# A fused linear-attention and MoE kernel: the first token block of expert 0 loaded as plain rows and turned on TensorE, and two second-visit scatters of group 1 put behind the last two of group 0

## The chip, the cores and the metric

The kernel runs on one core of a Trainium2 chip. The metric is the device time of one execution in microseconds (us); lower is better. A core has five engines with instruction streams of their own: PE (TensorE, matrix products), ACT (ScalarE), DVE (VectorE), POOL (GpSimd) and SP (SyncE, which here only issues transfers). Transfers run on 16 DMA engines. Each engine takes its instructions in the order of the program, so an instruction that waits holds back everything behind it on its engine.

## The reference

Linear attention without a causal mask, and a mixture of experts with noisy top-2 routing on its result:

```
q, k = phi(q), phi(k)                    # phi(x) = elu(x) + 1;  8 batches, 8 heads, 576 positions, 64 wide
kv = einsum('bhsd,bhse->bhde', k, v);  z = sum_s k
x = (q @ kv) / (q @ z + 1e-6)            # as 4608 tokens x 512
noisy = x @ w_gate + log1p(exp(x @ w_noise)) * noise        # 4608 x 8 experts
top2 = the two largest of a row;  w = softmax over these two
for e in range(8):                       # w1[e] 512 x 1024, w2[e] 1024 x 512
    for k in range(2):
        rows = top2[:, k] == e
        out[rows] += w[rows, k] * (relu(x[rows] @ w1[e]) @ w2[e])
```

`argpartition(-noisy, 2)` does not order the two best by their size: the kernel visits a token first for one of its two experts ("first visit", F) and then for the other ("second visit", S).

## The kernel before, in words

**Attention.** The batches go in four groups g = 0 to 3 of two. For a group, `K.g.h` are the kv products (L216, operand `e` = phi(k) and `v`), `V` their eviction into `kvbd` (L228), `T`/`t` a transpose of kv and its copy `kvt` (L235, L240), `U`/`u` the product with the router's weights and its copy (L246, L252). `Q.g.i` turns a piece of q on TensorE (L262) and `q.g.i` is ACT's copy of it to `pqt` (L267). `N.g.t` is the product of q with kv for a third t of the group (24 matmuls, L278), and `n.g.t.*` is DVE's work on it: the reciprocal of the denominator (L287, L289), the normalised rows into `xr` (L293) and the router's partial sums (L300).

**Routing.** Five units u (group 0, 1, 2, and group 3 in two parts). `R.u` is one step of the function `route`; it ends with the place of every token in a list in DRAM, `x_sorted`. `D.u.sl.ci` scatters 128 rows of unit u (1152 bytes each, sl = 0 first and 1 second visits) from `xr` to `x_sorted`: one indirect DMA of POOL (L413) and a memset behind it (L405). `xr` has three buffers, for groups 0 and 3, for group 1, and for group 2.

**Experts.** A block is a piece of one expert's list: "0a" is expert 0, first visits, tiles 0 and 1 (256 rows), "0b" its tiles 2 and 3, "1a" and "2a" the first of experts 1 and 2. `W.e.i` loads 1 MB of weights (L464, POOL), `M.k` the routing data of a block (L471, SP), `X.k` its rows (SP): turned by the transfer into `xt` (L615) or as rows `xn` (L617), according to the tuple `PLAIN`. A block of rows is turned on TensorE by `G.k.h` (L641, into PSUM, and a copy to `xt`, L645). `H.k.fc` is an eighth of the first product (4 matmuls, L697) and its ReLU on ACT (L699) into `hT`; `Y.k.t` is the second product of a tile (8 matmuls, L711), `y.k.t` its eviction on DVE (L723) and the store of it (L733).

**Order.** Everything up to expert 0's last block stands in one hand-written list of words, `SCRIPT`. Each word issues its instructions on all engines at once, and the order of the words is the order on each engine. At the word `^` the pools `A_kq` and `A_v` (q, k and v) are given back, and pools that are opened later lie in their place; at `|` the attention's pools go.

**PSUM.** Until `|` there are four small PSUM tiles of 2 KB per partition: two of the pool `ps_misc` (name `misc`) and two of `ps_b` (name `b`). `K`, `T`, `U`, `Q` and `R` take theirs from the method `misc()`, which gives the two pools in turn:

```
pool, name = self.ps_misc[self.turn % len(self.ps_misc)]
self.turn += 1
```

`H` and `Y` take theirs from `ps_b` alone, with the same buffers as the `b` of `misc()`. The word `one` makes `misc()` use `ps_misc` only from there on.

Of the kernel before, what the change touches and what calls it, by code (L numbers as in the profile page):

```python
# [860 lines left out]
R.2 n.2.2.2 R.2 R.2 R.2 R.2 R.2 t.3 m.q3.0 ^ X.0a W.1.1 D.1.0.8 D.1.1.5 D.1.0.3 D.1.0.7 D.1.0.4 D.1.1.3 D.0.1.7
D.0.1.8 H.0a.7 R.2 R.2 H.0a.2 H.0a.3 R.2 H.0a.4 Q.3.0 q.3.0 R.2 H.0a.5 U.3 u.3 Q.3.1 H.0a.0 H.0a.1 H.0a.6 R.2 R.2 R.2
q.3.1 R.2 R.2 R.2 n.2.2.1 R.2 N.3.0 R.2 R.2 R.2 Q.3.4 Q.3.2 q.3.2 R.2 R.2 R.2 Q.3.3 n.3.0.0 n.3.0.2 n.3.0.4 n.3.0.3
n.3.0.1 one D.1.1.4 D.2.1.1 D.2.0.7 D.2.0.6 D.2.1.0 D.2.0.0 W.2.0 D.2.0.5 N.3.1 R.2 M.2a X.0b X.1a q.3.3 H.0b.7 Y.0a.0
H.0b.0 q.3.4 n.3.1.0 n.3.1.2 n.3.1.4 R.2 n.3.1.1 n.3.1.3 X.2a M.0b y.0a.0 R.3 H.0b.6 N.3.2 H.0b.3 n.3.2.0 R.3 n.3.2.2
R.3 Y.0a.1 n.3.2.1 R.3 R.3 R.3 H.0b.2 R.3 y.0a.1 H.1a.2 H.1a.3 R.3 n.3.2.3 R.3 n.3.2.4 D.2.0.1 D.2.0.4 D.1.1.2 W.2.1 |
M.1a D.2.1.4 R.3 R.3 R.3 R.3 R.3 H.1a.0 H.0b.5 R.3 H.1a.4 R.3 R.3 R.3 H.0b.1 R.3 R.3 H.0b.4 R.3 R.3 R.3 R.3 R.3 R.3
H.1a.6 R.3 R.3 D.3.0.1 D.2.0.3 D.2.0.8 D.2.0.2 D.3.0.2 D.1.1.6 D.3.0.3 D.3.0.0 D.3.1.2 R.4 R.4 H.1a.5 R.4 R.4 Y.0b.1
Y.0b.0 R.4 R.4 R.4 H.2a.2 y.0b.0 y.0b.1 R.4 R.4 R.4 X.3a R.4 R.4 H.2a.0 R.4 H.1a.7 H.1a.1 R.4 R.4 H.2a.3 H.2a.1 Y.1a.0
R.4 X.0c Y.1a.1 H.2a.6 R.4 R.4 H.2a.5 R.4 y.1a.0 R.4 X.1b M.1b M.3a X.2b R.4 H.2a.4 R.4 R.4 R.4 H.2a.7 Y.2a.0 R.4 R.4  # L870
y.1a.1 M.0c y.2a.0 D.4.0.1 D.4.0.0 D.1.1.7 D.3.0.5 D.3.1.3 D.1.1.1 W.3.0 D.2.1.6 D.4.0.2 D.4.1.1 D.4.1.0 D.3.0.4
D.3.1.1 W.3.1 Y.2a.1 Y.1a.2 H.0c.5 M.2b y.2a.1 R.4 H.1b.3 H.1b.2 H.1b.4 H.0c.0 H.1b.7 H.0c.1 H.0c.3 H.0c.2 H.0c.4
H.0c.6 H.0c.7 X.0d G.2b.0 Y.0c.0 R.4 y.1a.2 Y.0c.1 y.0c.1 y.0c.0 H.1b.1 H.1b.6 H.1b.5 H.1b.0 H.2b.1 H.2b.4 H.2b.6
G.3a.0 Y.1b.1 Y.1b.0 H.2b.7 G.3a.1 H.2b.3 H.2b.0 H.3a.5 H.3a.1 H.3a.4 y.1b.1 y.1b.0 H.2b.5 H.2b.2 H.3a.3 Y.2b.0 G.0d.0
# [255 lines left out]
```

## Time and profile before

| | |
|---|---|
| median of 3 runs | 406.09 us (405.78 to 409.9) |
| profiled execution | 404.67 us, span 402.9 us |
| busy time, PE | 343.6 us (85% of the span) |
| busy time, POOL | 267.9 us (66%) |
| busy time, DVE | 186.0 us (46%) |
| busy time, ACT | 181.6 us (45%) |
| DMA | 85.60 MB, mean 212 GB/s |

The span runs from the first to the last instruction in the profile; the execution's own time has 1.8 us around it. Engines overlap, so the shares don't add up. "PEclk" is the clock that TensorE was granted, as a share of full speed. In a timeline a line is one or several instructions of one kind in a row; its first number is the start in us from the beginning of the span, the second how long they took. In brackets stands how long the engine was idle ahead of it, and what it waited for.

### The profile page before, as it was taken

Reading aid. Unit: us, or ns where it says so; the run is one execution under the profiler, and the core shown is the slowest. Engines: PE = TensorE matmul, PEld = TensorE weight load, DVE = VectorE, ACT = ScalarE, POOL = GpSimd, SP = SyncE. Lnnn points to the kernel's source line nnn. Section 1 sums busy time; section 2 is a strip of 40 time slices with the busy share of each in tenths; the row PEclk is TensorE's granted clock in tenths of the full one; section 3 lists DMA queues with packets and bytes.
Section 4 is the critical chain, followed back from the end, with each engine's and each line's share of the span. In section 5 each row is a group of like instructions: output and inputs, shape, how many; then the busy total and the mean of one; then the engine's idle time right before and its main releaser. Section 6 shows DMA issues by size and latency. Waiting matters only on the chain.

```text
span 402.9 us, 7018 instructions
## 1 busy us (share of the span) xinstructions
PE 343.6 (85%) x2527; PEld 204.1 (51%) x2557; DVE 186.0 (46%) x506; ACT 181.6 (45%) x342; POOL 267.9 (66%) x405
## 2 busy tenths in 40 slices
PE   6972757637378999989999999999999999999991
PEld 2452646526265657655566556545544544564440
DVE  3646969995839752331454233142224232343130
ACT  3279295765263525654444434443343334325410
POOL 8632327877878578846019397629878897898761
PEclk9968665888799999999999999999999999999997
DMA  8999999999979999995969999999999999963552
GB/s 128 204 207 205 231 215 209 240 219 251 198 184 203 294 290 223 200 358 154 207 182 156 179 228 202 201 241 184 276 229 253 226 197 274 266 195 135 164 205 83
DMA packets 81906, 85.60 MB, mean 212 GB/s; under 512 B 42911, under 2 KB 63074, under 8 KB 81862
## 3 DMA queue, kind: packets, MB, share of 16 engines
q0 software_dynamic: 34880, 63.92, 73.7%
q1 hardware_dynamic: 40310, 20.90, 24.4%
q10 hardware_dynamic: 6672, 0.24, 1.4%
q8 instruction: 22, 0.36, 0.4%
q14 instruction: 22, 0.18, 0.2%
HBM read 77.13 MB, written 33.79 MB: 275 GB/s over the span
## 4 chain that ended last, share of the span: by engine, by line
PE 61%; DMA 16%; POOL 7%; DVE 6%; ACT 5%; issue 3%; POOLq 0%; SPq 0%; DVEq 0%; ACTq 0%
PE b L697 30%; PE b L711 29%; POOL x_sorted L413 5%; DMA x_sorted<-xr 4%; DMA xt<-x_sorted 3%; ACT e L184 3%; DMA w<-in_moe_w_dram 2%; DMA xn<-x_sorted 2%; DMA kq<-in_q_dram 2%; DMA kq<-in_k_dram 2%; DVE e L196 1%; DVE xr L293 1%; ACT pqt L267 1%; PE t L641 1%; DVE kq L193 1%
## 5 line engine op out<-in xcount | busy, mean ns | idle before, releaser
L699 ACT ACTIVATE hT<-b 128x256 bf16<-128x256 f32 (+5 forms) x224 | 101.7, 461 | 140.8 <-PE b L697 132.5
L697 PE MATMUL b<-xt,w 128*128 128x256 bf16 (+5 forms) x890 | 147.4, 313 | 8.1 <-DMA xt<-x_sorted 6.4
L711 PE MATMUL b<-w,hT 128*128 128x512 bf16 (+1 forms) x616 | 141.4, 380 | 1.2
L697 PEld LDWEIGHTS <-w 128*128 128x128 bf16 x896 | 86.1, 99 | 61.6 <-issue 11.2
L413 POOL DMA_INDIRECT x_sorted<-xr x72 | 75.0, 1041 | 31.5 <-issue 11.7
L711 PEld LDWEIGHTS <-hT 128*128 128x128 bf16 (+1 forms) x640 | 59.1, 99 | 63.7 <-issue 1.9
L184 ACT ACTIVATE e<-kq 128x2304 bf16<-128x2304 bf16 x16 | 33.8, 2132 | 18.6 <-DMA kq<-in_q_dram 10.7
L739 POOL DMA_INDIRECT out_dram<-y,si x34 | 33.7, 992 | 11.5 <-DVE y L721 5.9
L677 POOL DMA_INDIRECT L<-part,gi x34 | 34.8, 1023 | 6.8 <-issue 6.5
L677 POOL DMA_INDIRECT L<-part,mgi x12 | 12.0, 1002 | 35.8 <-issue 24.5
L278 PE MATMUL num<-kvbd,pqt 128*64 128x162 bf16 x288 | 15.9, 270 | 15.2 <-DVE xr L293 10.0
L721 DVE SCALAR_TENSOR_TENSOR y<-b,mgate,L 128x512 f32<-128x512 f32 (+1 forms) x12 | 9.0, 746 | 39.5 <-DMA L<-part,mgi 16.6
L216 PE MATMUL b<-v,e 64*128 64x192 bf16 x144 | 17.9, 293 | 6.2 <-DVE e L196 5.0
L293 DVE TENSOR_TENSOR xr<-num,rden 128x768 bf16<-128x768 f32 x24 | 22.6, 947 | 0.1
L278 PEld LDWEIGHTS <-pqt 128*64 128x64 bf16 x288 | 12.8, 129 | 17.7 <-DVE xr L293 10.8
L196 DVE TENSOR_TENSOR e<-e,kq 128x2304 bf16<-128x2304 bf16 x16 | 21.2, 1348 | 0.1
L216 PEld LDWEIGHTS <-e 64*128 64x128 bf16 x288 | 15.6, 114 | 9.8 <-DVE e L196 6.4
L216 PE MATMUL misc<-v,e 64*128 64x192 bf16 x144 | 18.0, 291 | 1.4 <-DMA v<-in_v_dram 0.9
L170 POOL DMA_DIRECT2D v<-in_v_dram x20 | 12.8, 654 | 9.5 <-DMA kq<-in_q_dram 4.7
L721 DVE SCALAR_TENSOR_TENSOR y<-b,meta7S,L 128x512 f32<-128x512 f32 (+1 forms) x10 | 7.5, 749 | 22.9 <-PE b L711 17.1
L155 PE MATMUL num<-ones 128*128 128x512 bf16 x52 | 14.2, 443 | 3.6 <-DVE ones L66 3.6
L746 POOL MEMSET gap<- 128x416 f32 x36 | 16.8, 467 | 0.0
(189 smaller groups left out, 345.9 us busy)
## 6 DMA issues: line engine op xcount, KB each, us to landing
w<-in_moe_w_dram POOLq DMA_DIRECT2D x16, 1024.0 KB, 11.3
part<-y SPq DMA_DIRECT2D x39, 256.0 KB
kq<-in_k_dram POOLq DMA_DIRECT2D x6, 576.0 KB
kq<-in_q_dram POOLq DMA_DIRECT2D x6, 576.0 KB
v<-in_v_dram POOLq DMA_DIRECT2D x12, 288.0 KB, 16.7
kq<-in_k_dram POOLq DMA_DIRECT2D x4, 288.0 KB
v<-in_v_dram POOLq DMA_DIRECT2D x8, 144.0 KB, 7.6
kq<-in_q_dram POOLq DMA_DIRECT2D x4, 288.0 KB
```

The costliest lines, as they stand in the source:

```text
L184: self.nc.scalar.activation(out=e, in_=x, func=ACT.Exp)
L196: nc.vector.tensor_tensor(out=e, in0=e, in1=x, op=ALU.min)
L216: nc.tensor.matmul(out=self.kvps[g, h, j][:, KVM * i : KVM * i + KVM], lhsT=e[half, hp, ci, :], rhs=v[half, hp + 8 - step : hp + 9 + step ...
L278: self.nc.tensor.matmul(out=ps[half, hp, KVW * i : KVW * i + KVW], lhsT=self.pqt[g, 3 * t + i][:, hp, half], rhs=self.kvbd[g % 2][:, j, hp ...
L293: nc.vector.tensor_tensor(out=_ap(xr, [[64, 4], [ROW_W, 3], [1, 64]], off=3 * t * ROW_W + 256 * s), in0=_ap(ps, [[512, 4], [KVW, 3], [1, 6 ...
L413: r = self.nc.gpsimd.indirect_dma_start(out=self.x_sorted, out_offset=bass.IndirectOffsetOnAxis(ap=row[:, HD // 2 + 3 + sl : HD // 2 + 4 + ...
L677: r = nc.gpsimd.indirect_dma_start(out=L[0:m].bitcast(INT32), out_offset=None, in_=self.part.bitcast(INT32), in_offset=bass.IndirectOffset ...
L697: nc.tensor.matmul(out=ps[:, 0:n], lhsT=w1[:, dc, units], rhs=b["xt"][:, dc, 0:n], start=(dc == 0), stop=(dc == 3))
L699: nc.scalar.activation(out=b["hT"][:, fc, 0:n], in_=ps[:, 0:n], func=ACT.Relu)
L711: nc.tensor.matmul(out=ps[i * m : i * m + m], lhsT=b["hT"][:, f, t * P : t * P + m], rhs=w2[:, f, :], start=(fc == 0), stop=(fc == 8 // n ...
L739: r = nc.gpsimd.indirect_dma_start(out=self.out, out_offset=bass.IndirectOffsetOnAxis(ap=self.m[e, kind, i]["si"][0:m], axis=0), in_=y[0:m ...
L746: nc.gpsimd.memset(self.c["gap2"][:], 0.0)
```

## The change

Block "0a" joins `PLAIN`: its 256 rows come as rows (`xn`, in a new pool `B_n0` with one buffer, opened behind `^` on the right side) and are turned by a new word `G.0a.0` ahead of `H.0a.7`. TensorE's pool `ps_t` does not exist there yet, so `xn_t` takes its PSUM tile from `misc()`. `M.0a` moves from before `K.2.0` to behind `^`, `X.0a` from right behind `^` to behind the ten scatters that follow it, and `D.1.1.5` and `D.1.1.3` move behind `D.0.1.7` and `D.0.1.8`.

```
 x_load
-            b["xn"] = self.np.tile([P, 4, HD], BF16, name="xn")
+            b["xn"] = (self.np.tile([P, 4, HD], BF16, name="xn") if self.np else self.np0.tile([P, 3, HD], BF16, name="xn"))
 xn_t
-        ps = self.ps_t.tile([P, 2, 4, P], BF16, name="t")[:]
+        if self.ps_t:
+            ps = self.ps_t.tile([P, 2, 4, P], BF16, name="t")[:]
+        else:
+            ps = self.misc()[:].bitcast(BF16).rearrange("p (i c r) -> p i c r", i=2, c=4)
 SCRIPT
-... W.0.1 M.0a K.2.0 ...
-... t.3 m.q3.0 ^ X.0a W.1.1 D.1.0.8 D.1.1.5 D.1.0.3 D.1.0.7 D.1.0.4 D.1.1.3 D.0.1.7
-D.0.1.8 H.0a.7 R.2 R.2 H.0a.2 H.0a.3 R.2 H.0a.4 Q.3.0 q.3.0 ...
+... W.0.1 K.2.0 ...
+... t.3 m.q3.0 ^ M.0a W.1.1 D.1.0.8 D.1.0.3 D.1.0.7 D.1.0.4 D.0.1.7 D.0.1.8 D.1.1.5
+D.1.1.3 X.0a G.0a.0 H.0a.7 R.2 R.2 H.0a.2 H.0a.3 R.2 H.0a.4 Q.3.0 q.3.0 ...
...
-PLAIN = ("2b", "3a", "0d")
+PLAIN = ("0a", "2b", "3a", "0d")
+NB0 = 1
...
                 pb.wp.append(right("B_w2", 3))
+                pb.np0, pb.misc = right("B_n0", NB0), pa.misc
```

On SP, the loads of block 0a's routing data and rows, with the semaphores that each waits for (the number is the same in all of them; `DMAHW` and `DMASW` are transfers). Before:

```order
L471 DMA meta0F_918<-x_sorted 128x2x4 [waits DMASW6_49,DMASW7_49,DMASW5_49,DMAHW1_49,DMASW3_49,DMASW2_49]
L615 DMA_TRANSPOSE xt<-x_sorted 128x4x256 [waits DMAHW2_49]
L471 DMA meta2F_1691<-x_sorted 128x2x4 [waits DMASW6_49,DMASW5_49,DMASW7_49,DMASW4_49,DMAHW3_49,DMASW3_49,DMASW2_49]
L615 DMA_TRANSPOSE xt<-x_sorted 128x4x256 [waits DMAHW4_49]
L615 DMA_TRANSPOSE xt<-x_sorted 128x4x384 [waits DMAHW5_49]
```

and now:

```order
L471 DMA meta0F_1440<-x_sorted 128x2x4 [waits DMASW6_49,DMASW7_49,DMASW5_49,DMAHW1_49,DMASW3_49,DMASW2_49]
L617 DMA xn<-x_sorted 128x2x512 [waits DMAHW2_49,DMASW4_49,PE_49]
L471 DMA meta2F_1705<-x_sorted 128x2x4 [waits DMASW6_49,DMASW5_49,DMASW7_49,DMASW4_49,DMAHW3_49,DMASW3_49,DMASW2_49]
L615 DMA_TRANSPOSE xt<-x_sorted 128x4x256 [waits DMAHW4_49]
L615 DMA_TRANSPOSE xt<-x_sorted 128x4x384 [waits DMAHW5_49]
```

The routing data keeps its place and its waits. The load of the rows is another kind of transfer and has two more waits: one for a transfer of POOL, and one for TensorE (the PE count in question is that of the last matmul of `K.3.1`, which reads `v`, in whose space `xn` lies).

On ACT, from the first ReLU of block 0a to those of `H.0b` (the three `L267` copies in it that have 1024 columns and stand behind the first are `q.3.1`, `q.3.2`, `q.3.3`); the word behind `<-` says which PSUM pool is read. Before, the row ahead of these is the copy `t.3` (`kvt`):

```order
L699 ACTIVATE hT<-b 128x256 x4
L267 COPY pqt<-misc 128x1024
L699 ACTIVATE hT<-b 128x256
L252 CAST kvbd_115<-b 128x8x32
L699 ACTIVATE hT<-b 128x256 x3
L267 COPY pqt<-misc 128x1024
L376 ACTIVATE xr_179<-ge 128x2x9
L377 ACTIVATE xr_179<-tokid 128x9
L267 COPY pqt<-b 128x1024
L267 COPY pqt<-misc 128x1024
L699 ACTIVATE hT<-b 128x256 x2
L267 COPY pqt<-misc 128x512
```

and now, behind the same copy `t.3` (the lines of the file have shifted by 3):

```order
L648 COPY xt<-misc 128x2x4x128
L702 ACTIVATE hT<-b 128x256 x4
L267 COPY pqt<-b 128x1024
L702 ACTIVATE hT<-b 128x256
L252 CAST kvbd_115<-misc 128x8x32
L702 ACTIVATE hT<-b 128x256 x3
L267 COPY pqt<-b 128x1024
L376 ACTIVATE xr_179<-ge 128x2x9
L377 ACTIVATE xr_179<-tokid 128x9
L267 COPY pqt<-misc 128x1024
L267 COPY pqt<-b 128x1024
L702 ACTIVATE hT<-b 128x256 x2
```

One copy is new, ahead of the first ReLU of the block. The order behind it is the same, but each tile of `misc()` has changed its pool, since one more call was made: those of `Q.3.0`, `Q.3.1` and `Q.3.3` (and of `Q.3.4`, whose copy follows the last row here) lie in `b` now, which the products of `H` and `Y` use too, and those of `U.3`, `R.2` and `Q.3.2` in `misc`.

On PE, the last matmul of `H.0b.7`, the first two of `Y.0a.0`, and the first of `H.0b.0` seven matmuls later. Before:

```order
L697 MATMUL b<-xt,w_838 128x256
L711 LDWEIGHTS hT [waits DMASW1_49]
L711 MATMUL b<-w_839,hT 128x512 [waits DVE_49]
L711 LDWEIGHTS hT
...
L697 LDWEIGHTS w_838
L697 MATMUL b<-xt,w_838 128x256 [waits Activation_49]
```

and now:

```order
L700 MATMUL b<-xt,w_838 128x256
L714 LDWEIGHTS hT [waits DMASW1_49]
L714 MATMUL b<-w_839,hT 128x512 [waits Activation_49]
L714 LDWEIGHTS hT
...
L700 LDWEIGHTS w_838
L700 MATMUL b<-xt,w_838 128x256 [waits DVE_49]
```

The two waits have changed places: `Y.0a.0` now waits for an instruction of ACT (the ReLU of `H.0b.7`), and `H.0b.0` for one of DVE (the eviction `y.0a.0` of the tile that `Y.0a.0` has just filled).

## Rows read from the trace of the kernel before

**Rows 1.** Windows: PE, PEld, DVE, ACT, POOL busy (instructions); granted clock; DMA share; GB/s.

```profile
95.00:107.00 12.00, 4.58 (x92) 3.43 (x86) 10.48 (x25) 3.65 (x11) 10.58 (x16) 0.91 1.16 197
107.00:120.00 13.00, 10.19 (x114) 8.12 (x116) 6.88 (x23) 7.31 (x15) 9.73 (x19) 0.82 0.80 191
120.00:147.00 27.00, 25.72 (x202) 16.07 (x203) 20.45 (x82) 11.41 (x33) 19.34 (x36) 1.00 1.02 251
...
176.00:260.00 84.00, 83.53 (x542) 48.45 (x549) 30.53 (x113) 37.89 (x83) 46.77 (x65) 1.00 0.99 201
```

**Rows 2.** The same columns, three short stretches around block 0a's start.

```profile
101.00:104.00 3.00, 0.00 (x0) 0.00 (x0) 2.96 (x5) 1.54 (x3) 2.65 (x4) 1.00 0.84 129
104.00:107.00 3.00, 0.00 (x0) 0.00 (x0) 2.79 (x9) 0.00 (x0) 2.63 (x5) 0.64 1.02 240
107.00:111.00 4.00, 3.90 (x22) 2.88 (x23) 2.92 (x13) 1.45 (x4) 3.44 (x7) 0.50 1.10 238
```

**Rows 3.** The chain that ended last: start, us, what.

```profile
86.26 8.60 DMA x_sorted<-xr
...
95.48 11.48 DMA xt<-x_sorted
...
147.26 0.97 POOL x_sorted L413
...
165.74 9.95 DMA xn<-x_sorted
...
175.73 0.62 PE t L641 x8
```

**Rows 4.** Timeline of PE from K.3.1's last matmul to N.3.2.

```profile
98.93 0.24 PE L216 MATMUL misc<-v,e 64*128 64x192 bf16 x1
...
107.10 3.57 PE L697 MATMUL b<-xt,w 128*128 128x256 bf16 x16 [6.41 <-DMA xt<-x_sorted]
...
112.13 0.61 PE L262 MATMUL misc<-ident,e 128*128 128x128 bf16 x8
112.91 1.67 PE L697 MATMUL b<-xt,w 128*128 128x256 bf16 x12 [0.17 <-ACT hT L699]
...
115.95 0.90 PE L278 MATMUL num<-kvbd,pqt 128*64 128x162 bf16 x20 [0.72 <-ACT pqt L267]
...
121.27 1.89 PE L711 MATMUL b<-w,hT 128*128 128x512 bf16 x7
123.00 0.60 PE L697 MATMUL b<-xt,w 128*128 128x256 bf16 x4
124.07 0.60 PE L697 MATMUL b<-xt,w 128*128 128x256 bf16 x4 [0.47 <-ACT hT L699]
124.60 1.04 PE L278 MATMUL num<-kvbd,pqt 128*64 128x162 bf16 x24
```

**Rows 5.** Timeline of ACT: copies kvt, q.3.0, q.3.1, and a later block's xt.

```profile
102.47 1.01 ACT L240 COPY kvt<-b 128x1024 bf16<-128x1024 bf16 x1
...
111.56 1.01 ACT L267 COPY pqt<-misc 128x1024 bf16<-128x1024 bf16 x1 [0.47 <-PE misc L262]
...
114.89 1.01 ACT L267 COPY pqt<-misc 128x1024 bf16<-128x1024 bf16 x1
...
176.39 1.01 ACT L645 COPY xt<-t 128x1024 bf16<-128x1024 bf16 x1 [2.92 <-PE t L641]
```

**Rows 6.** Timeline of DVE around y.0a.0.

```profile
124.70 0.75 DVE L723 TENSOR_SCALAR y<-b,meta0F 128x512 f32<-128x512 f32 x1
...
125.83 0.17 DVE L287 TENSOR_SCALAR rden<-num 128x24 f32<-128x24 f32 x1
```

**Rows 7.** Timeline of POOL: two weight loads.

```profile
102.34 0.81 POOL L464 DMA_DIRECT2D w<-in_moe_w_dram  x1
...
163.16 0.96 POOL L464 DMA_DIRECT2D w<-in_moe_w_dram  x1
```

**Rows 8.** Tile x_sorted, 90 to 130 us: its transfers' times to landing.

```profile
DMA to landing us min/median/max: 4.2/7.3/10.3
```

More of the change, by code (lines that the diff above doesn't have):

```diff
@@ L854 @@
 D.0.1.1 D.0.1.4 D.0.1.0 D.0.0.3 W.0.0 n.1.0.0 R.0 e.q2.1 n.1.0.1 n.1.0.4 n.1.0.3 n.1.0.2 N.1.1 m.k2.0 m.k2.1 D.0.0.8
-D.0.0.4 D.0.0.7 l.q3 D.0.0.2 q.1.4 e.q2.0 q.1.3 W.1.0 D.0.1.5 D.0.0.5 D.0.1.3 D.0.0.6 D.0.1.2 W.0.1 M.0a K.2.0 n.1.1.0
+D.0.0.4 D.0.0.7 l.q3 D.0.0.2 q.1.4 e.q2.0 q.1.3 W.1.0 D.0.1.5 D.0.0.5 D.0.1.3 D.0.0.6 D.0.1.2 W.0.1 K.2.0 n.1.1.0
 n.1.1.4 n.1.1.2 n.1.1.3 n.1.1.1 r.q2 N.1.2 K.2.1 V.2.1 e.k3.1 R.0 m.q2.1 m.q2.0 n.1.2.0 n.1.2.4 n.1.2.3 R.1 R.1 V.2.0
@@ L860 @@
 n.2.1.1 n.2.1.2 n.2.1.4 n.2.1.3 N.2.2 e.q3.1 K.3.1 n.2.2.0 V.3.0 V.3.1 R.1 n.2.2.3 r.q3 n.2.2.4 R.2 R.2 R.2 m.q3.1 T.3
[L861 to L874, printed above, removed]
@@ L875 @@
-Y.2b.1 D.4.1.2 D.2.1.5 D.3.1.5 D.2.1.3 D.2.1.7 y.2b.1 D.1.1.8 D.2.1.2 D.2.1.8 D.3.1.0 D.3.1.4 G.0d.1 H.3a.7 mids
-y.2b.0 H.3a.0 H.3a.2 prep H.3a.6
+R.2 n.2.2.2 R.2 R.2 R.2 R.2 R.2 t.3 m.q3.0 ^ M.0a W.1.1 D.1.0.8 D.1.0.3 D.1.0.7 D.1.0.4 D.0.1.7 D.0.1.8 D.1.1.5
+D.1.1.3 X.0a G.0a.0 H.0a.7 R.2 R.2 H.0a.2 H.0a.3 R.2 H.0a.4 Q.3.0 q.3.0 R.2 H.0a.5 U.3 u.3 Q.3.1 H.0a.0 H.0a.1 H.0a.6
+R.2 R.2 R.2 q.3.1 R.2 R.2 R.2 n.2.2.1 R.2 N.3.0 R.2 R.2 R.2 Q.3.4 Q.3.2 q.3.2 R.2 R.2 R.2 Q.3.3 n.3.0.0 n.3.0.2
+n.3.0.4 n.3.0.3 n.3.0.1 one D.1.1.4 D.2.1.1 D.2.0.7 D.2.0.6 D.2.1.0 D.2.0.0 W.2.0 D.2.0.5 N.3.1 R.2 M.2a X.0b X.1a
@@ new lines @@
+q.3.3 H.0b.7 Y.0a.0 H.0b.0 q.3.4 n.3.1.0 n.3.1.2 n.3.1.4 R.2 n.3.1.1 n.3.1.3 X.2a M.0b y.0a.0 R.3 H.0b.6 N.3.2 H.0b.3
+n.3.2.0 R.3 n.3.2.2 R.3 Y.0a.1 n.3.2.1 R.3 R.3 R.3 H.0b.2 R.3 y.0a.1 H.1a.2 H.1a.3 R.3 n.3.2.3 R.3 n.3.2.4 D.2.0.1
+D.2.0.4 D.1.1.2 W.2.1 | M.1a D.2.1.4 R.3 R.3 R.3 R.3 R.3 H.1a.0 H.0b.5 R.3 H.1a.4 R.3 R.3 R.3 H.0b.1 R.3 R.3 H.0b.4
+R.3 R.3 R.3 R.3 R.3 R.3 H.1a.6 R.3 R.3 D.3.0.1 D.2.0.3 D.2.0.8 D.2.0.2 D.3.0.2 D.1.1.6 D.3.0.3 D.3.0.0 D.3.1.2 R.4 R.4
+H.1a.5 R.4 R.4 Y.0b.1 Y.0b.0 R.4 R.4 R.4 H.2a.2 y.0b.0 y.0b.1 R.4 R.4 R.4 X.3a R.4 R.4 H.2a.0 R.4 H.1a.7 H.1a.1 R.4
@@ new lines @@
+R.4 H.2a.3 H.2a.1 Y.1a.0 R.4 X.0c Y.1a.1 H.2a.6 R.4 R.4 H.2a.5 R.4 y.1a.0 R.4 X.1b M.1b M.3a X.2b R.4 H.2a.4 R.4 R.4
+R.4 H.2a.7 Y.2a.0 R.4 R.4 y.1a.1 M.0c y.2a.0 D.4.0.1 D.4.0.0 D.1.1.7 D.3.0.5 D.3.1.3 D.1.1.1 W.3.0 D.2.1.6 D.4.0.2
+D.4.1.1 D.4.1.0 D.3.0.4 D.3.1.1 W.3.1 Y.2a.1 Y.1a.2 H.0c.5 M.2b y.2a.1 R.4 H.1b.3 H.1b.2 H.1b.4 H.0c.0 H.1b.7 H.0c.1
+H.0c.3 H.0c.2 H.0c.4 H.0c.6 H.0c.7 X.0d G.2b.0 Y.0c.0 R.4 y.1a.2 Y.0c.1 y.0c.1 y.0c.0 H.1b.1 H.1b.6 H.1b.5 H.1b.0
+H.2b.1 H.2b.4 H.2b.6 G.3a.0 Y.1b.1 Y.1b.0 H.2b.7 G.3a.1 H.2b.3 H.2b.0 H.3a.5 H.3a.1 H.3a.4 y.1b.1 y.1b.0 H.2b.5 H.2b.2
@@ L877 @@
+H.3a.3 Y.2b.0 G.0d.0 Y.2b.1 D.4.1.2 D.2.1.5 D.3.1.5 D.2.1.3 D.2.1.7 y.2b.1 D.1.1.8 D.2.1.2 D.2.1.8 D.3.1.0 D.3.1.4
+G.0d.1 H.3a.7 mids y.2b.0 H.3a.0 H.3a.2 prep H.3a.6
 """
```

## The prediction, made before the changed kernel ran

> **What bounds the kernel now.** I read the windows first. From 120 us on TensorE is the bound: 25.72 of 27 us busy, and 83.53 of 84 in a long stretch later [rows 1]. A delay of TensorE's queue before 120 us can hardly be won back behind it. The stretch from 95 to 107 us is different: PE is busy for 4.58 of 12 us [rows 1], and from 101 to 107 us it does nothing at all [rows 2]. The chain of waits names the reason: the last scatter that block 0a needs lands at 86.26 + 8.60 = 94.86, the turned load of its rows then takes from 95.48 to 106.96, 11.48 us [rows 3], and the first product of 0a starts at 107.10 after 6.41 us of idleness [rows 4]. So a quicker load of these rows is worth something at this place, up to the next thing that is late. The clock adds to it: after the idle time TensorE has a granted clock of 0.64 and then 0.50, its lower level of 1.2 GHz, until 111 us [rows 2].
>
> Behind this place the chain crosses to POOL at 147.26 (scatters of the next unit), to a load and back to PE at 175.73 [rows 3]. Those scatters follow routing steps whose matmuls stand in PE's queue, so the later crossing moves with PE and doesn't absorb a shift made earlier.
>
> **The turned load becomes a row load.** It can't start at 95.48. The new buffer lies where v was, and the load waits for the last matmul on v, which ends at 98.93 + 0.24 = 99.17 [rows 4]; that gives 99.3 for the issue. The other new wait is for a transfer of POOL's, older than this matmul by all I can see. How long 256 KB of rows take here no row shows. From below: the shortest transfer on x_sorted in this stretch landed 4.2 us after its issue [rows 8]. From above: a row load further on took 9.95 us [rows 3], behind a weight load issued at 163.16, 2.6 us before it [rows 7]. Here the next weight load is issued 3 us after the row load (102.34 [rows 7]), so I take the end with no load just ahead, 4.2 us: landing at 103.5. Both ends stay in the range.
>
> The Trainium skill says something on this (DMA: Bandwidth & Descriptors, section "Queues, rings and completion order"): a DMA engine goes round the queues that have work, one packet at a time, so a load on SP's queue would share with a weight load on POOL's and not stand behind it. That speaks for the short end; the 9.95 us row is against reading it as free of cost.
>
> **The turn on TensorE.** It is new work: 8 transposes at 0.62 us [rows 3] and a copy of 1.01 us on ACT [rows 5], 1.7 us with the starts between them (PE to ACT to PE, some 0.05 each). ACT is free, since the copy of kvt ends at 102.47 + 1.01 = 103.48 [rows 5], before the transposes do. So the first product starts at 103.5 + 1.75 = 105.25 in place of 107.10: **1.85 us earlier**. With an even earlier landing the copy couldn't start before 103.48, which makes 104.5 and 2.6 us the most that can be gained here.
>
> The Trainium skill prices a 128x128 transpose higher (TensorE: Matmul & The Clock Gate, section "Part 4: PE-mode transpose"): about 275 ns each in one kernel. Eight would take 2.2 us as an estimate, and 1.6 us of the gain would go. The row of eight in 0.62 us decides here, because it is the same line with the same shape.
>
> **One more call of misc().** The diff doesn't show this part, the order of instructions does. Since the pools are handed out in turn, one more call swaps the pool of every tile behind it until the word "one". Three things follow.
>
> First, Q.3.0 takes a `b`, so Q.3.1, also in `b`, needs q.3.0's copy done. That copy ends at 111.56 + 1.01 = 112.57 [rows 5]; Q.3.1 started at 112.13 [rows 4] and now starts at 112.61, all on the clock of before. The next product (H.0a.0, 112.91, after 0.17 us of idleness [rows 4]) slips by 0.14 only, to 113.05.
>
> Second, the tile of Q.3.1 now holds one of the two `b` until q.3.1, so H.0a.0, H.0a.1 and H.0a.6 go through one buffer, each waiting for the ReLU of the one before. What that pitch is the trace shows later: two products of 0.60 us at 123.00 and 124.07 with an idle 0.47 us between them, a pitch of 1.07 [rows 4]. So they start at 113.05, 114.12 and 115.19. Before, the twelve matmuls of the three took from 112.91 to 114.58 [rows 4], that is the third started at about 113.98. It is 1.21 us late, and the ReLU, the copy q.3.1 (114.89 [rows 5]) and N.3.0 behind it (115.95, waiting for that copy [rows 4]) are late by the same: **1.2 us lost**. DVE's normalisation and N.3.1 follow N.3.0, so up to there the balance is 1.85 - 1.2 = 0.65 us to the good.
>
> Third, at the end of group 3 the tiles of Q.3.3 and Q.3.4 are both in `b`. H.0b.7, Y.0a.0 and H.0b.0 then share what is left, one buffer. Y.0a.0 has to wait for the ReLU of H.0b.7, and, what costs more, H.0b.0 for the eviction y.0a.0. DVE does that at 124.70 for 0.75 us, behind the normalisation of N.3.1 [rows 6], and its order isn't changed. H.0b.0 started at 123.00 [rows 4]; it would now start at 124.70 + 0.75 + 0.05 = 125.50, 2.5 us later. Queued behind it on PE are H.0b.6 and N.3.2 (124.60 [rows 4]); DVE waited for N.3.2 to start its next rden at 125.83 [rows 6], with some 0.1 us of other work in between: **2.4 us lost**. The wait of Y.0a.0 lies inside this one: its last 7 matmuls take 1.89 us from 121.27 [rows 4], and even 0.6 us later they end before DVE comes to the tile.
>
> **The moved scatters and M.0a.** Ten scatters stand on POOL before and after, with the same memsets, so POOL ends at the same time; D.0.1.7 and D.0.1.8 come two places earlier, D.1.1.5 and D.1.1.3 two later. Nobody near waits for any of them: the routing data and the blocks that follow read first visits. D.1.0.4, for which the loads of 0b, 1a and 2a wait, comes one place earlier, and those loads were in time. M.0a keeps its place and waits on SP. I cost all of it at nothing; what hides it is that SP and POOL have these lists landed before PE asks, and if that cover were gone it would be one scatter's place, at about 1.3 us (0.97 us [rows 3], a memset and a start).
>
> **The clock.** I put it at nothing, with two bounds. If TensorE doesn't fall to its lower level because it waits less, the 3.90 busy us between 107 and 111 us at a granted 0.50 [rows 2] take half: 1.95 us gained. If the new idle time ahead of H.0b.0, about 2 us, makes it fall once more, as much is lost.
>
> **The sum.** -1.85 + 1.2 + 2.4 = +1.75 us on the profiled 404.67, that is 406.4; the median of the runs shown stands 1.42 us over that execution, so 406.09 + 1.75 = **407.8**.
>
> **The rivals.**
>
> *Slower: the row load lands late.* If it shares the DMA engines with what is queued there, as the load at 165.74 did with its 9.95 us [rows 3], it lands at 109.2, and 0a starts at 110.95, 3.85 us late where I have 1.85 early: 5.7 us more, 413.5. It passes 1% from a landing at about 105.8 on. For it: the DMA engines are as busy from 104 to 107 us (share 1.02) as anywhere [rows 2], and the longest transfer of the tile took 10.3 us [rows 8]. Against it: from 101 to 104 the share is 0.84 [rows 2], that stretch held the turned load, which is gone, and the weights of 102.34 come after it. 0.15.
>
> *Faster: the buffers' waits are covered.* The load lands by 102.5 (2.6 us gained), the clock doesn't fall (1.95), and the pair of 1.2 and 2.4 us remains: -0.95. If two holes of PE's queue as long as the one of 0.47 us ahead of H.0b.6 [rows 4] take up 0.94 of the last, it is -1.9: 404.2. For it: such holes are there. Against it: a gain at the head is worth little while y.0a.0 holds PE. 0.2, and it passes 1% only if the waits on `b` cost nothing at all.
>
> *A second fall of the clock.* PE idles ahead of H.0b.0, and falls as it did in the 6.41 us ahead of 0a: 1.95 more, about 409.8. Against it: that hole is a third as long. 0.10.
>
> **How the numbers follow.** The forecast, 406.5 to 409.5, has 0.55. The range takes in the faster rival and the second fall and part of the late load: 404.0 to 411.0. One per cent, 4.06 us, is about what a measurement of this kernel can tell from no change (its three runs lie 4.1 us apart). Faster by more than that, below 402.0: 0.06. Slower, above 410.15: most of the late load and half of the second fall, 0.17. Within: 0.77.
>
> **What the profile of after would show.** The row load issued near 99.3 and landed near 103.5; eight transposes and a copy ahead of the first product, at 105.2; a pitch of 1.07 us between H.0a.0, H.0a.1 and H.0a.6 with PE idle for ACT's ReLU; N.3.0 at about 115.3; a hole of nearly 2 us ahead of H.0b.0 that ends with DVE's y; N.3.2 near 126.4, and everything from there 1.7 us late, with as little idle time as before. What would prove me wrong: a landing after 105 us, a DVE that comes to y.0a.0 sooner, or a shift at 130 us that is gone at 260.

## The result and the profile after

The changed kernel took 408.22 us (median, 406.31 to 416.93) against 406.63 us (402.2 to 413.42) for the kernel before, twenty executions each: the medians lie 1.6 us apart. The ratio is 1.0078 with a 95% interval of 1.0049 to 1.0107, that is 3.2 us slower, between 2.0 and 4.4. This ratio, like those of the experiments below, counts only the executions within 1.5% of the fastest of the same kernel, and so leaves out six of the twenty before and one of the twenty changed, which is why it is larger than the distance of the medians. The direction is the same in both; the size is 1.6 or 3.2 us by the two ways of counting, one per cent at most but for the end of the interval. The forecast was +1.75 us and a median of 407.8.

The profiled execution of the changed kernel took 412.23 us with a span of 410.4, and was one of the longer ones (the profile before is of an execution of 404.67 us). Its stretch before the change already ran 1.64 us later (the last matmul of K.3.1 starts at 100.57 where it was 98.93 [rows 4]), so I read every time below from that matmul's start, written +x. The last two columns are runs that come later in this text.

| from the last matmul of K.3.1 | before | changed | changed, no swap of pools | before, with the swap alone |
|---|---|---|---|---|
| first product of 0a | +8.17 | +7.32 | +7.43 | +7.81 |
| N.3.0, its 20 matmuls | +17.02 | +17.40 | +16.23 | +17.26 |
| H.0b.0 | +24.07 | +26.94 | +23.50 | +26.81 |
| first routing matmul of unit 3 (L359) | +33.79 | +37.83 | +33.06 | +37.58 |
| ratio to the kernel before | | 1.0078 | 1.0012 | 1.0148 |

The first of the routing products, 9.72 us behind H.0b.0 in the kernel before, is this row of its timeline:

```profile
132.72 0.21 PE L359 MATMUL misc<-A,ut 128*128 128x96 bf16 x1
```

Four of the twelve experiments ran beside a kernel before of 407.56 us (median of 29). The other eight ran on two chips on which the kernel before itself took 449.8 and 444.1 us; the intervals of their ratios are mostly wider than the effect, and I take from them only which wait stands where, and the time between two near places.

The timeline of PE in the changed kernel, the same places as [rows 4]; the first number is the start, the second how long the line's instructions took, and in brackets stands the idle time ahead and what ended it:

```profile
100.57 0.24 PE L216 MATMUL misc<-v,e 64*128 64x192 bf16 x1
...
105.78 1.01 PE L644 MATMUL misc<-ident,xn 128*128 128x128 bf16 x8 [3.45 <-DMA xn<-x_sorted]
107.89 3.57 PE L700 MATMUL b<-xt,w 128*128 128x256 bf16 x16 [1.10 <-ACT xt L648]
...
114.93 0.60 PE L700 MATMUL b<-xt,w 128*128 128x256 bf16 x4 [0.47 <-ACT hT L702]
116.00 0.60 PE L700 MATMUL b<-xt,w 128*128 128x256 bf16 x4 [0.47 <-ACT hT L702]
...
117.97 0.90 PE L278 MATMUL num<-kvbd,pqt 128*64 128x162 bf16 x20 [0.72 <-ACT pqt L267]
...
123.92 1.89 PE L714 MATMUL b<-w,hT 128*128 128x512 bf16 x8 [0.47 <-ACT hT L702]
127.51 0.60 PE L700 MATMUL b<-xt,w 128*128 128x256 bf16 x4 [1.70 <-DVE y L726]
...
129.10 1.72 PE L278 MATMUL num<-kvbd,pqt 128*64 128x162 bf16 x24
...
138.40 0.21 PE L359 MATMUL misc<-A,ut 128*128 128x96 bf16 x1
```

Ahead of the first product there is new work: eight transposes (L644) from 105.78, then a wait for ACT's copy, then the sixteen matmuls at 107.89, 2.1 us later. At 114.93 and 116.00 the products wait 0.47 us each for a ReLU, where [rows 4] has twelve matmuls in one row. And H.0b.0 at 127.51 waits 1.70 us for DVE's `y`, a wait that the kernel before doesn't have.

The chain of waits of the changed kernel shows the same two places, and with them the load itself:

```profile
100.87 4.77 DMA xn<-x_sorted
...
106.83 1.02 ACT xt L648
...
126.71 0.76 DVE y L726
```

Of windows (columns as in [rows 1]) the three in the first list answer to [rows 1]; those in the second are shorter, the first two of them as in [rows 2]:

```profile
95.00:107.00 12.00, 8.09 (x120) 6.57 (x117) 10.22 (x25) 3.95 (x13) 10.36 (x16) 0.78 0.83 194
...
120.00:147.00 27.00, 22.11 (x170) 13.81 (x169) 19.18 (x70) 11.10 (x28) 16.95 (x31) 0.94 0.89 212
...
176.00:260.00 84.00, 83.32 (x545) 48.31 (x545) 29.09 (x109) 37.76 (x84) 44.43 (x65) 1.00 0.97 210
```

```profile
104.00:107.00 3.00, 1.01 (x8) 0.88 (x9) 2.86 (x8) 1.27 (x3) 2.51 (x5) 0.73 0.60 115
107.00:111.00 4.00, 3.11 (x15) 2.22 (x15) 3.72 (x12) 1.96 (x4) 3.44 (x7) 0.50 1.05 163
...
120.00:124.00 4.00, 1.75 (x31) 1.33 (x30) 3.01 (x8) 1.99 (x3) 3.38 (x7) 1.00 0.92 211
124.00:128.00 4.00, 2.30 (x12) 1.09 (x12) 3.71 (x11) 0.00 (x0) 3.51 (x6) 1.00 0.83 182
128.00:147.00 19.00, 18.05 (x129) 11.38 (x128) 12.46 (x52) 9.11 (x25) 10.06 (x20) 0.91 0.90 219
```

PE is now busy for 8.09 of the 12 us up to 107 (before 4.58). Only 1.01 us of that are the new transposes; most of the rest is the work of `K.3`, which in this execution ran later and at a lower clock (0.36 us for one of its products, 0.24 at the end). From 120 PE is busy for 22.11 of the 27 us (before 25.72). The clock is at 0.73 and 0.50 around 0a's start, much as it was (0.64 and 0.50). New is that it falls again: PE is busy for 1.75 and 2.30 of two stretches of 4 us, and from 128 the granted clock is 0.91, where the kernel before has 1.00 throughout. From 176 us on PE is as full as it was (83.32 of 84).

### The profile page after: what moved, and what is told of

The parts are those of the page before. It is cut to its first block, busy times and chain, and to the rows that moved or that the text cites. A ratio compares the mean times of both kernels' runs of the same rounds, so it can differ in the third digit from the quotient of the medians.

```text
span 410.4 us, 7068 instructions
## 1 busy us (share of the span) xinstructions
PE 345.6 (84%) x2565; PEld 204.8 (50%) x2565; DVE 185.8 (45%) x506; ACT 182.4 (44%) x343; POOL 266.9 (65%) x405
## 3 DMA queue, kind: packets, MB, share of 16 engines
HBM read 77.39 MB, written 33.79 MB: 271 GB/s over the span
## 4 chain that ended last, share of the span: by engine, by line
DMA 35%; PE 30%; POOL 20%; issue 7%; DVE 3%; ACT 2%; POOLq 1%; DVEq 0%; SPq 0%; ACTq 0%
PE b L700 14%; PE b L714 12%; DMA kq<-in_q_dram 9%; DMA v<-in_v_dram 8%; POOL L L680 6%; DMA part<-y 5%; POOL out_dram L742 5%; POOL x_sorted L413 4%; DMA xn<-x_sorted 3%; DMA L<-part,mgi 3%; DMA L<-part,gi 2%; DMA x_sorted<-xr 2%; POOL gap L688 2%; DMA kq<-in_k_dram 2%; POOL gap L749 2%
## 5 line engine op out<-in xcount | busy, mean ns | idle before, releaser
L714 PE MATMUL b<-w,hT 128*128 128x512 bf16 (+1 forms) x640 | 143.4, 381 | 2.4 <-DVE y L724 2.0
L216 PE MATMUL b<-v,e 64*128 64x192 bf16 x144 | 19.1, 306 | 6.2 <-DVE e L196 5.0
L216 PEld LDWEIGHTS <-e 64*128 64x128 bf16 x288 | 16.6, 119 | 12.0 <-DVE e L196 8.5
L216 PE MATMUL misc<-v,e 64*128 64x192 bf16 x144 | 19.3, 306 | 3.4 <-DVE e L196 2.5
L193 DVE TENSOR_SCALAR kq<-kq 128x4608 bf16<-128x4608 bf16 (+1 forms) x10 | 11.3, 1126 | 12.1 <-ACT e L184 12.0
```

The source lines that it names most:

```text
L216: nc.tensor.matmul(out=self.kvps[g, h, j][:, KVM * i : KVM * i + KVM], lhsT=e[half, hp, ci, :], rhs=v[half, hp + 8 - step : hp + 9 + step ...
L714: nc.tensor.matmul(out=ps[i * m : i * m + m], lhsT=b["hT"][:, f, t * P : t * P + m], rhs=w2[:, f, :], start=(fc == 0), stop=(fc == 8 // n ...
```

## The experiments

**The theory** to test is the prediction's: the row load gains a little at 0a's start, and the one more call of `misc()` loses more, in two places. The rival is that the row load and its turn cost the time themselves, and the pools are only a change of names.

**No swap.** A word `flip` adds one to the turn, behind the transposes:

```
+    def do_flip(self):
+        self.pa.turn += 1
-... D.1.1.3 X.0a G.0a.0 H.0a.7 ...
+... D.1.1.3 X.0a G.0a.0 flip H.0a.7 ...
```

> The changed kernel, but the turn of the two PSUM pools is set back behind the new transposes, so that every later tile of misc() lies in the pool that it had before. All times from the start of K.3.1's last matmul (before: first product of 0a at +8.17, N.3.0 at +17.02, H.0b.0 at +24.07, routing product of unit 3 at +33.79; after: +7.32, +17.40, +26.94, +37.83). Theory 1, the swap of pools costs all that is lost: first product at +7.3 as after, N.3.0 at +16.2, H.0b.0 at +23.2, no wait of H.0b.0 for DVE's y, routing product at +32.9; the run some 0.9 us under the kernel before, ratio about 0.998. Rival, the row load and its turn on TensorE themselves cost the time (transfers in the way, a copy on ACT): routing product later than +36 and a ratio of 1.005 or more.

Beside the kernel before of 449.8 us it took 451.88 us, ratio 1.0261 (1.0126 to 1.0397), useless for the time. H.0b.0 waited 2.81 us there for a ReLU and not for `y`. The same kernel once more, beside one of 407.56 us:

> The kernel of the first run once more, because the chip of that call took 450 us for the kernel before and its intervals are wider than the effect. The changed kernel with the turn of the PSUM pools set back behind the new transposes. From the start of K.3.1's last matmul: Theory 1, the swap costs all that is lost: first product of 0a at +7.3, N.3.0 at +16.2, H.0b.0 at +23.2 without a wait for y, routing product of unit 3 at +32.9, ratio 0.998. Rival, the row load and the turn cost the time: routing product later than +36, ratio 1.005 or more.

405.28 us (402.79 to 410.18), ratio 1.0012 (0.9970 to 1.0054): the changed kernel's loss is gone, though the two intervals touch (1.0049 to 1.0107 there). The timeline of PE:

```profile
98.00 0.24 PE L216 MATMUL misc<-v,e 64*128 64x192 bf16 x1
...
103.32 1.01 PE L644 MATMUL misc<-ident,xn 128*128 128x128 bf16 x8 [3.56 <-DMA xn<-x_sorted]
105.43 3.57 PE L700 MATMUL b<-xt,w 128*128 128x256 bf16 x16 [1.10 <-ACT xt L648]
...
114.23 0.90 PE L278 MATMUL num<-kvbd,pqt 128*64 128x162 bf16 x20 [0.72 <-ACT pqt L267]
...
121.50 0.60 PE L700 MATMUL b<-xt,w 128*128 128x256 bf16 x4
...
123.10 1.04 PE L278 MATMUL num<-kvbd,pqt 128*64 128x162 bf16 x24
...
131.06 0.21 PE L359 MATMUL misc<-A,ut 128*128 128x96 bf16 x1
```

The places come out as the theory said: +7.43, +16.23, +23.50 and +33.06, against +7.3, +16.2, +23.2 and +32.9. H.0b.0 at 121.50 waits for nothing, and N.3.2 at 123.10 takes 1.04 us, the clock not lower. The rival had the routing product later than +36; it falls.

**The swap alone.** The kernel before, with nothing but

```
-... D.0.1.8 H.0a.7 ...
+... D.0.1.8 flip H.0a.7 ...
```

> The kernel before with the turned load and nothing changed but the turn of the two PSUM pools, moved on by one ahead of H.0a.7. Theory 1: N.3.0 1.2 us and H.0b.0 3.7 us later than before against K.3.1 (+18.2 and +27.8), routing product at +38 or more, ratio about 1.010 to 1.012, higher than the change's 1.0078. Rival, the row load costs the time: N.3.0 at +17.0, routing product at +33.8, ratio 1.000.

Beside the kernel before of 449.8 us it took 450.33 us, ratio 1.0220 (1.0092 to 1.0348); H.0b.0 waited for `y`. And beside the one of 407.56 us:

> The kernel of the second run once more, for the same reason: the kernel before with nothing changed but the turn of the two pools. Theory 1: N.3.0 at +18.2, H.0b.0 at +27.8 behind a wait for y.0a.0, routing product at +38 or more, ratio 1.010 to 1.012. Rival: N.3.0 at +17.0, routing product at +33.8, ratio 1.000.

410.46 us (408.51 to 414.13), ratio 1.0148 (1.0094 to 1.0202): the swap alone is enough for the whole loss. That it costs more than the change does is not shown: the two intervals overlap, and its routing product comes at +37.58, 0.25 us sooner than in the changed kernel. The timeline of PE:

```profile
99.58 0.24 PE L216 MATMUL misc<-v,e 64*128 64x192 bf16 x1
...
107.39 3.25 PE L697 MATMUL b<-xt,w 128*128 128x256 bf16 x16 [6.05 <-DMA xt<-x_sorted]
...
113.80 0.60 PE L697 MATMUL b<-xt,w 128*128 128x256 bf16 x4 [0.47 <-ACT hT L699]
114.86 0.60 PE L697 MATMUL b<-xt,w 128*128 128x256 bf16 x4 [0.47 <-ACT hT L699]
...
116.84 0.90 PE L278 MATMUL num<-kvbd,pqt 128*64 128x162 bf16 x20 [0.72 <-ACT pqt L267]
...
126.39 0.60 PE L697 MATMUL b<-xt,w 128*128 128x256 bf16 x4 [1.71 <-DVE y L723]
...
128.40 1.83 PE L278 MATMUL num<-kvbd,pqt 128*64 128x162 bf16 x24
...
137.16 0.21 PE L359 MATMUL misc<-A,ut 128*128 128x96 bf16 x1
```

H.0b.0 comes behind the wait for `y` of 1.71 us, N.3.2 takes 1.83 in place of 1.04 us, and the routing product is at +37.58. N.3.0 was expected at +18.2 and is at +17.26: 0a starts 0.36 us sooner here than in the profile before, and the lower clock ended sooner too (the transposes of Q.3.0 take 0.61 us, before 1.06). The two products with their waits of 0.47 us are there.

**The two halves of the swap.** First half alone: the turn set back ahead of Q.3.4. Second half alone: set back behind the transposes and moved on again ahead of Q.3.4.

```
+... X.0a G.0a.0 H.0a.7 ... flip Q.3.4 Q.3.2 ...         (first half)
+... X.0a G.0a.0 flip H.0a.7 ... flip Q.3.4 Q.3.2 ...    (second half)
```

> The changed kernel with the turn set back ahead of Q.3.4: only the first half of the swap is left (Q.3.0, U.3, Q.3.1, R.2). Theory 1: N.3.0 at +17.4 as after, but H.0b.0 at +24.4 with no wait for y.0a.0, no second fall of the clock behind it, routing product at +34.2; ratio 1.000 to 1.002. Rival, the late part of the loss comes from elsewhere (scatters moved, loads of 0b late): H.0b.0 still at +26 or later, ratio 1.005 to 1.008.

> The changed kernel with the turn set back behind the new transposes and moved on again ahead of Q.3.4: only the second half of the swap is left (Q.3.4, Q.3.2, Q.3.3). Theory 1: N.3.0 at +16.2, H.0b.0 at +25.7 behind a wait for y.0a.0 of some 1.7 us, routing product at +36.6 if the clock falls again and +35.4 if not; ratio 1.004 to 1.007. Rival, the waits on buffers are hidden by others: routing product at +33.5, ratio 0.998 to 1.000.

> The third kernel of the first call once more: only the first half of the swap (Q.3.0, U.3, Q.3.1, R.2 in the other pool), the turn set back ahead of Q.3.4. Runs so far gave, from the start of K.3.1's last matmul, for the kernel with no swap: first product of 0a +7.43, N.3.0 +16.23, H.0b.0 +23.50, routing product +33.06. Theory 1: first product +7.4, N.3.0 +17.4 (1.2 us more, from the pitch of 1.07 us in one buffer), H.0b.0 +24.7 without a wait for y, routing product +34.3; ratio 1.002 to 1.005. Rival, the first half is hidden: the same as with no swap.

> The fourth kernel of the first call once more: only the second half of the swap (Q.3.4, Q.3.2, Q.3.3 in the other pool). Theory 1: N.3.0 +16.2 as with no swap, H.0b.0 +25.8 behind a wait for y.0a.0 of 1.7 us, the clock lower behind it, routing product +36.5; ratio 1.006 to 1.010. Rival, the wait for y is filled by others: routing product at +33.5 or before, ratio 1.002 or less.

All four ran on the two slower chips: first half 449.32 us, ratio 1.0099 (0.9769 to 1.0430), and 447.35, 1.0155 (1.0081 to 1.0229); second half 446.71, 1.0131 (1.0008 to 1.0253), and 449.28, 1.0154 (1.0031 to 1.0277). These don't price the halves. The places against K.3.1 are shifted by holes ahead of 0a that have nothing to do with them. And the halving has a wait of its own, in all four and in no other run: with the turn moved between R.2 and Q.3.4, Q.3.3 has to wait until DVE has read the tile of R.2 (2.44 us, at 133.46 below), and N.3.1 comes 4.66 to 5.08 us behind N.3.0 in place of 3.90. From the first product of 0a to N.3.0 there is no such hole, and the distance is the first half's own: 8.80 us with no swap, 10.08 in the changed kernel, 10.08 in both runs of the first half, 9.00 and 8.86 in those of the second. Of the second runs, PE at the products in one buffer and at H.0b.0, the first half first:

```profile
126.30 0.60 PE L700 MATMUL b<-xt,w 128*128 128x256 bf16 x4 [0.47 <-ACT hT L702]
127.37 0.60 PE L700 MATMUL b<-xt,w 128*128 128x256 bf16 x4 [0.47 <-ACT hT L702]
...
133.46 0.62 PE L262 MATMUL misc<-ident,e 128*128 128x128 bf16 x8 [2.44 <-DVE tot L388]
...
140.06 0.60 PE L700 MATMUL b<-xt,w 128*128 128x256 bf16 x4 [1.14 <-ACT hT L702]
```

```profile
122.68 1.67 PE L700 MATMUL b<-xt,w 128*128 128x256 bf16 x12
...
140.87 1.01 PE L700 MATMUL b<-xt,w 128*128 128x256 bf16 x4 [0.84 <-DVE y L726]
```

With the first half there are the waits of 0.47 us, and H.0b.0 waits for a ReLU; with the second there is one row of twelve matmuls, and H.0b.0 waits for `y`. That wait is 0.84 us where 1.7 was expected, since there `Y.0a.0` itself waited 2.84 and 4.30 us for the ReLU of H.0b.7. So each half makes the wait that was put down to it. What the second costs on a chip like that of the result was not measured apart.

**The rows earlier.** With room of their own (2 KB per partition, found by letting the router's staging tile lie in the zero row's), the load has no wait for K.3.1; it is issued, turned and copied right behind T.3:

```
-            b["xn"] = ... self.np0.tile([P, 3, HD], BF16, name="xn"))
+            b["xn"] = ... self.np0.tile([P, 2, HD], BF16, name="xn"))     # np0: left side, opened first
-... T.3 R.2 n.2.2.2 ... ^ M.0a W.1.1 ... D.1.1.3 X.0a G.0a.0 H.0a.7 ...
+... T.3 M.0a X.0a G.0a.0 flip R.2 n.2.2.2 ... ^ W.1.1 ... D.1.1.3 H.0a.7 ...
```

> The row load with no swap, with room of its own for the rows (2 KB per partition, taken from the routers' staging tile's side of memory), and loaded and turned right behind T.3: the load needs no wait for K.3.1, the copy goes ahead of kvt's on ACT. Theory 1, the row load is worth what its start allows: first product of 0a at +3 in place of +8.17, the clock not lower there, N.3.0 at +13 to +14; then H.0b.7 waits for the rows of 0b, whose load hangs on the scatters of unit 1 and comes only 1 us sooner (+20.5), so that N.3.2 and the routing product come 1 to 2 us sooner than before (+32), ratio 0.995 to 0.998. Rival, the head gives nothing since DVE's chain (phi of q, routing of unit 2) sets N.3.0: N.3.0 at +16.5 or later.

405.82 us (403.28 to 409.20) beside 407.56, ratio 1.0021 (0.9983 to 1.0059). The load's issue on SP, and PE at 0a's start and at H.0b.7:

```profile
95.74 0.46 SPq L617 DMA_DIRECT2D xn<-x_sorted  x1
```

```profile
103.08 1.03 PE L644 MATMUL misc<-ident,xn 128*128 128x128 bf16 x8 [2.85 <-DMA xn<-x_sorted]
105.22 1.01 PE L700 MATMUL b<-xt,w 128*128 128x256 bf16 x4 [1.10 <-ACT xt L648]
106.58 2.72 PE L700 MATMUL b<-xt,w 128*128 128x256 bf16 x12 [0.35 <-ACT kvt L240]
...
114.30 0.90 PE L278 MATMUL num<-kvbd,pqt 128*64 128x162 bf16 x20 [0.72 <-ACT pqt L267]
...
119.57 0.96 PE L700 MATMUL b<-xt,w 128*128 128x256 bf16 x4 [0.32 <-DMA xt<-x_sorted]
```

Neither theory had this: the first product came at +6.74 and N.3.0 at +15.82, where the one had +3 and +13 to +14 and the other N.3.0 at +16.5 or later. The load was issued 2.74 us ahead of K.3.1's last matmul (98.48 here), where with no swap it came 0.30 us behind it: 3.0 us sooner. But its transposes start at +4.60, only 0.7 us sooner than with no swap (+5.32): from issue to transposes it took 7.3 us in place of 5.0. The first four matmuls then ran, and the next had to wait for the copy of kvt, which holds a `b` (0.35 us). At the far end H.0b.7 (119.57) waited for the rows of 0b, as expected, and its four matmuls took 0.96 in place of 0.60 us, at a lower clock (0.67 from 119 to 121 us, 0.50 from there to 123). The routing product came at +34.51, later than with no swap and than in the kernel before.

**The weights out of the way.** The run before and W.1.1 behind four scatters, so that the turned loads of 0b, 1a and 2a come sooner:

```
-... ^ W.1.1 D.1.0.8 D.1.0.3 D.1.0.7 D.1.0.4 D.0.1.7 ...
+... ^ D.1.0.8 D.1.0.3 D.1.0.7 D.1.0.4 W.1.1 D.0.1.7 ...
```

> As the third run of this call, and the weight load W.1.1 moved on POOL from ahead of the four scatters D.1.0.8, D.1.0.3, D.1.0.7 and D.1.0.4 to behind them, so that the rows of 0b, 1a and 2a can be loaded some 4 us sooner. Theory 1: H.0b.7 right behind N.3.1, no wait for rows; N.3.2 and the routing product 4 us sooner than before (+29.8), ratio about 0.990. Rival, what is won at the head is given back by another wait (expert 1's second weights, now late, or DVE): routing product at +32 or later, or ratio 0.996 or more.

412.82 us (406.26 to 420.26) beside 407.56, ratio 1.0086 (1.0030 to 1.0141): slower. The profiled execution took 416.44 us. The weight load on POOL, the three turned loads on SP, and PE at H.0b.7:

```profile
108.99 0.81 POOL L464 DMA_DIRECT2D w<-in_moe_w_dram  x1
```

```profile
111.06 13.59 SPq L615 DMA_TRANSPOSE xt<-x_sorted  x3
```

```profile
124.18 1.03 PE L700 MATMUL b<-xt,w 128*128 128x256 bf16 x4 [3.07 <-DMA xt<-x_sorted]
```

The turned loads are issued from 111.06, +10.92, where the run before had them at +15.97, and take 13.59 us to issue in place of 5.44. The weight load went out 2.1 us ahead of them here (108.99); H.0b.7 waits 3.07 us for the rows, and the routing product comes at +38.07, where +29.8 was foretold. The rival is right that what was won is given back by another wait, though it is not one of the two that it named. Whether the other executions had it too was not measured.

**The weights farther out of the way, and TensorE kept busy.** Two runs beside the kernel before of 444.1 us: no swap and W.1.1 behind all ten scatters, and the same with 13 matmuls of 512 columns on constants while TensorE waits for the rows of 0a.

```
+            raw, ones = self.misc(), self.c["ones"]
+            for _ in range(13):
+                nc.tensor.matmul(out=raw[:], lhsT=ones[:], rhs=_ap(ones, [[0, 4], [1, P]]), start=True, stop=True)
```

> The changed kernel with no swap, and the weight load W.1.1 behind all ten scatters that followed it. In the run that put it behind four of them the turned loads of 0b, 1a and 2a took 13.6 us to issue, beside that load. Theory 1, the load collided with the turned ones: with it out of their way the first of them lands by +18, H.0b.7 follows N.3.1 without a wait, and nothing else is late: N.3.0 at +16.2, H.0b.0 at +23.5, routing product at +33, ratio 0.997 to 1.001, and no long issue of the turned loads (under 6 us). Rival, any delay of W.1.1 makes the turned loads slow: H.0b.7 waits for rows past +22, routing product at +35 or more, ratio 1.005 or more.

> As the third run of this call, and 13 matmuls of 512 columns on constants into the PSUM tile of the turn, ahead of the eight transposes, in the time in which TensorE waits for the rows of 0a (work that the reference does not need; its result is overwritten). Theory 1: the granted clock stays at 1 over the first products of 0a, the transposes take 0.62 us and the sixteen matmuls 1.8 us in place of 3.57, N.3.0 at +14.4 in place of +16.2, and with rows of 0b landed early the gain stays: routing product at +31.3, ratio 0.993 to 0.997. Rival, DVE's chain or the rows of 0b take it back: routing product at +32.8, ratio as without the matmuls.

454.97 us, ratio 1.0234 (1.0067 to 1.0400), and 450.97, 1.0251 (1.0170 to 1.0333): neither is faster, and more than that these two don't say of the time. In the first the weight load went out 6.5 us ahead of the turned loads (113.30 and 119.77), which took 5.11 us to issue, and H.0b.7 followed N.3.1 without a wait, as foretold. N.3.0 came at +14.83. H.0b.0 then waited 2.86 us for a ReLU, as with no swap on the other slow chip, and the routing product came at +39.39, far behind the +33 foretold. The second shows the clock, on PE from T.3 to the first products:

```profile
117.41 3.76 PE L642 MATMUL misc<-ones 128*128 128x512 bf16 x13
121.10 0.61 PE L647 MATMUL misc<-ident,xn 128*128 128x128 bf16 x8
122.81 2.10 PE L703 MATMUL b<-xt,w 128*128 128x256 bf16 x16 [1.10 <-ACT xt L651]
```

```profile
117.00:119.00 2.00, 2.00 (x11) 0.76 (x8) 1.93 (x4) 0.00 (x1) 0.00 (x0) 0.50 1.07 192
119.00:121.00 2.00, 2.00 (x10) 0.78 (x8) 1.97 (x4) 1.36 (x3) 0.00 (x0) 0.99 1.18 282
121.00:124.00 3.00, 1.86 (x19) 1.41 (x19) 2.86 (x7) 1.70 (x4) 0.00 (x0) 1.00 1.29 200
```

The granted clock, 0.50 from 117 to 119 us, is 0.99 and 1.00 behind that, while the 13 matmuls run; the transposes take 0.61 us (1.01 in the changed kernel), the sixteen matmuls 2.10 (3.57). N.3.0 comes at +14.19, 0.64 us sooner than in the run before, though the transposes start 0.98 us later (+5.50 against +4.52), right behind the last of the 13. The routing product is where it was, at +39.38. Whether it would pay on a chip like that of the result, with the rows of 0b the next thing late, stays open.

## Why the prediction was right

The direction, the range and the mechanism held; one term was too large and one that stood at nothing had a size. Both go the same way, so that the forecast of +1.75 us is 2.3 short of the one execution's 4.04: that the median of 408.22 lies 0.4 us from the 407.8 forecast is in part luck, the more so as the median before rose from 406.09 to 406.63 with more executions.

- **The turned load becomes a row load, and the turn:** forecast -1.85, measured 8.17 - 7.32 = -0.85. The load was issued right at the end of K.3.1, as foretold (100.81, and 100.87 on SP), and landed in 4.77 us where I took 4.2. The transposes took 1.01 us and not 0.62, since I priced them by a row at full clock though the clock was falling there. These two make up all but a few hundredths of the 1.0 us. The Trainium skill's price (TensorE: Matmul & The Clock Gate, "Part 4: PE-mode transpose"), 2.2 us for eight as an estimate, is above the measured 1.01 us too. The size of the gain is uncertain by some 0.4 us: the kernel with the swap alone keeps the turned load and has its first product at +7.81, so that by this pair the gain is 0.49 us there and gone at the routing product (+37.58, and +37.83 with the row load). By the pair without the swap it is 0.74 and 0.73.
- **One more call of misc(), up to N.3.0:** forecast +1.2, measured 0.38 + 0.85 = +1.23, with the pitch of 1.07 us (113.86, 114.93, 116.00). The distance from the first product to N.3.0 in the two halves confirms it.
- **H.0b.0 behind y.0a.0:** forecast 2.5 at H.0b.0, measured 2.87 - 0.38 = 2.49. It ends with DVE's `y` at 127.46, and the 0.47 us that Y.0a.0 waits for a ReLU lie inside it, as foretold. That DVE waited for N.3.2 at 125.83, by which I made 2.4 of it, is not in [rows 6]: no idle time stands ahead of that instruction.
- **The clock:** forecast 0 with bounds of 1.95 us, measured +1.17, which is what is added from H.0b.0 (+2.87) to the routing product (+4.04). It is the rival of the second fall, at 0.10 in the forecast, and it came in the profiled execution, in that of the swap alone, and not in that without the swap. What I had against it, that the hole is a third as long as the one ahead of 0a, did not hold: behind 1.70 us the clock fell. The 1.17 us are net: the product at 133.86 is 1.61 us late by it, and the row of 24 matmuls behind wins 0.44 back. That the wait for `y` brings the fall here is argued from these two pairs. It is not the only wait that does: on one of the slower chips the kernel with no swap has H.0b.0 and H.0b.6 behind waits of 2.81 and 3.72 us for a ReLU, and N.3.2 takes 1.83 us there too; and in the run with the rows earlier the clock was lower at H.0b.7.
- **The moved scatters and M.0a:** forecast 0. With no swap they are moved as well, and the routing product comes at +33.06, 0.73 us sooner than before; they are not tested apart, and a cost of a few tenths could hide in it.
- **To the end:** the 4.04 us stand unchanged at the second routing product (+46.58, now +50.62) and at the first transposes behind it (+57.97, now +62.01). At the load that the chain crosses at 175.73 [rows 3] a part is absorbed, against the forecast: TensorE waits 0.68 us there where it was 1.06, and 3.65 us are left. They are still there at 260 us (a transpose at +156.53, now +160.19). The rest of the 7.5 us between the two spans is the 1.64 us of the start and 2.2 us behind 260, where the changed kernel waits 0.37 and 1.60 us for DVE's `y` and the kernel before doesn't; the medians, 1.6 us apart, don't have it.

The sum by these terms is -0.85 + 1.23 + 2.49 + 1.17 = +4.04 us in the one execution; the ratio of the runs says 3.2, 2.0 to 4.4, and their medians 1.6. The late load, which I gave 0.15, stayed away: its landing at 105.64 is 4.77 us after the issue. The forecast's sign of being wrong, a landing after 105, and its point of decision, 105.8, stand against a K.3.1 that ended 1.64 us sooner; counted from K.3.1 as there, it landed at 104.0.

Left open are what the row load is worth by itself in time (ratio 1.0012, 0.9970 to 1.0054, where one pair of traces has 0.7 us and the other none), the price of the second half of the swap apart, and whether any version beats the kernel before: no ratio here is below 1, though the medians with no swap and with the rows earlier lie 2.3 and 1.7 us under that of the kernel before.

## What to carry to other kernels

Where buffers are handed out in turn from two pools, one more call shifts every later tile; look at which later instructions then share a buffer, since an edit in one place can cost its time 20 us behind. A row load that replaces a turned one can be worth less than the load's difference: here 4.77 in place of 11.48 us of transfer gave 0.85 at the first product, since the turn, the copy and the wait for the space came back on the path. Price an operation by a row at the clock that holds where it will stand.
